# 240 rows to an expert, weight pieces set between the rows, block 1 gathered in the first MoE, single idle products

## The chip, the cores and the metric

The kernel runs on one core of a Trainium2 chip. The core has five engines that run side by side and wait for each other by semaphores: TensorE (PE; its weight loads are listed as PEld), VectorE (DVE), ScalarE (ACT), GpSimd (POOL) and SyncE (SP), from whose queue nearly all DMAs are issued; POOL issues the indexed ones. The metric is the device time of one launch in microseconds, as the median of a few runs.

## The reference

Three layers in a row over 3072 tokens (4 sequences of 768) of 384 numbers. Cut to what is computed:

```python
# gated linear attention, 8 heads of 48
state = f[:, :, t, :, None] * state + einsum('bhd,bhe->bhde', k[:, :, t], v[:, :, t])
y[:, :, t] = einsum('bhd,bhde->bhe', q[:, :, t], state)
# first MoE: 8 experts, 384 -> 1024 -> 384; a token goes to one expert or to none
do_compute = x @ w_skip > 0
e_idx = argmax(xc @ w_gate); gate_w = softmax(xc @ w_gate)[e_idx]
out[do_compute] = xc + gate_w * (maximum(xc @ w1[e], 0) @ w2[e])
# second MoE: dense, 384 -> 2048 -> 384
h = x @ w_in
g = where(h >= 1, h, where(h <= -1, 0, (h + 1) ** 2 / 4))
return g @ w_out
```

The weights of the second MoE arrive as 64-bit floats.

## The kernel before

Tokens stand in 24 tiles of 128 rows. Every float32 product that needs it is made of three fp32r products, high by high, high by low and low by high (`PASS`, `ORDER`), so that each operand is kept as an upper half (made by ACT) and a lower half (made by DVE or POOL as the difference).

Attention runs in an order written out by hand (`PLAN`). It ends with the routing of the last three tiles (21 to 23), one by one: logits on PE, choice of the expert on DVE, rank by PE, place on DVE. Meanwhile POOL has sent the rows of the earlier tiles by indexed DMA into `xs_d`, 256 rows (`CAP`) for each of 8 experts; a token whose rank in its expert is not under the limit is counted in `over`. Tokens of the first six tiles have a lower limit, 128 (`CAP0`), so that their rows stand in the first half of an expert's share. Ten calls of `warm` in the plan put products of the identity matrix on PE that nothing reads. At the end all engines read a flag (line 931): if a token is over the limit, a slow branch computes it; otherwise the branch is jumped over.

The first MoE (`moe1`) takes expert after expert: for 8 blocks of 128 hidden units nine products each (line 1132), streaming the expert's 256 rows; from PSUM ACT makes the upper half of h, DVE the lower (lines 1135, 1136); then for two tiles of 128 rows 24 products of 384 columns (line 1151), and ACT copies the result (`yo`), which goes to `yb_d`. The second MoE (`moe2`) takes blocks of three tiles, b = 0 to 7, twice: first the hidden blocks f = 0 to 7, then 8 to 15. A step (b, f) is nine products of layer 1 (line 1227), the bend by ACT and DVE into gh and gl, and, three steps later, nine products of layer 2 (line 1282).

All other work is strewn among these products by a clock of ticks: 16 in an expert, so 128 in the first MoE, and two in a step of the second. At a tick every job that runs does its next step, and its instructions go into the engines' queues, which keep their order. Three kinds of job matter here. `split_job` loads a piece of w1 or w2 (ACT line 251, DVE line 254). `widen_job` turns a piece of 384 columns of the 64-bit weights into float32: a load, `mag` on ACT (line 286), five DVE steps (lines 291 to 301), and then either a store, or the upper half by ACT (line 307) and the lower by POOL (line 311). Pieces of the second kind are the 20 of `DIRECT`; the list `direct` has the ticks at which they start, `direct_steps` at which tick after its start each of the six steps stands. `combine_job(b)` brings the expert's results back to the tokens of block b: an indexed gather by POOL (line 1181), gate and sum by DVE (line 1187), a store, a load in turned order, a 32x32 transpose by DVE (line 1202), upper half by ACT, lower half by POOL (lines 1208, 1212). `rows` has the steps of the second MoE at which it starts for b = 1 to 7. Block 0 is handled apart: its rows are gathered in the first MoE without the last expert (`base_job`), and the last expert's part is added through PE (`patch`), after the second layer's first tile of that expert.

Of the kernel before, what the change touches and what calls it, by code (L numbers as in the profile page):

```python
# [11 lines left out]
F32 = mybir.dt.float32  # L12
F32R = mybir.dt.float32r
# [17 lines left out]
CAP0 = 128  # L31
HOT = 21
# [25 lines left out]
    "rows": [0, 7, 15, 23, 31, 39, 47],  # L58
# [113 lines left out]
def gla_moe_kernel(ctx: ExitStack, tc: tile.TileContext, a: dict, out: bass.AP):  # L172
# [165 lines left out]
    def route_group(i0, n, ps_x, rt, tag, dense=False, cap=CAP, hot=None, ranks=None):  # L338
# [138 lines left out]
    def attention():  # L477
        with ExitStack() as es:
# [202 lines left out]
            def clear_rows(z):  # L681
                nc.sync.dma_start(z, zt[:z.shape[0]])
# [77 lines left out]
            for g, (i0, n) in enumerate(((0, 6), (6, 6), (12, 6), (18, 3), (21, 1), (22, 1), (23, 1))):  # L760
                job = route_group(i0, n, ps_x, rt, "x", cap=CAP if g else CAP0, hot=hot if i0 >= HOT else None,
# [251 lines left out]
    def moe1():  # L1013
        with ExitStack() as es:
# [5 lines left out]
            def load_x(e):  # L1020
                if e >= E:
                    return
                xg_t[e] = [mx.tile([128, DM], F32, tag="xg", name="xg", bufs=XG) for t in range(2)]
                for t in range(2):
                    nc.sync.dma_start(xg_t[e][t], xs_d[CAP * e + 128 * t:CAP * e + 128 * t + 128, :])

            def prep_x(e):
                xg = xg_t.pop(e)
                xh, xl = xhl[e] = x_pair(hp_, CAP)
                for t in range(2):  # L1030
                    tp = ps_t.tile([128, 3, 128], F32, tag="tp", name="tp")
                    for c in range(3):
                        T.transpose(tp[:, c], xg[t][:, 128 * c:128 * (c + 1)], ident)
                    sl = slice(128 * t, 128 * t + 128)
                    A.activation(xh[:, :, sl], tp, AF.Copy)
                    V.tensor_tensor(out=xl[:, :, sl], in0=tp, in1=xh[:, :, sl].bitcast(F32), op=ALU.subtract)
# [74 lines left out]
            agenda.setdefault(MTUNE["select"], []).append(select_job)  # L1111
            for i in range(TB):
# [9 lines left out]
            for e in range(E):  # L1122
# [4 lines left out]
                hs = [hp_.tile([128, 8, CAP], F32R, tag=f"h{z}", name=f"h{z}") for z in range(2)]  # L1127
# [18 lines left out]
                for t in range(2):  # L1146
# [12 lines left out]
                    A.activation(yo, op, AF.Copy)  # L1159
                    store = lambda e=e, t=t, yo=yo: nc.sync.dma_start(  # L1160
                        yb_d[CAP * e + 128 * t:CAP * e + 128 * t + 128, :], yo)
# [5 lines left out]

    def moe2():
        NF = F2 // 128
        with ExitStack() as es:  # L1170
            gp = es.enter_context(tc.tile_pool(name="gp", bufs=2))
            gs, ops, post = {}, {}, []

            def combine_job(b):
                tiles, t = range(TB * b, TB * (b + 1)), {}

                def gather(i):
                    t["g", i] = mx.tile([128, DM], F32, tag="xg", name="xg", bufs=XG)  # L1180
                    G.indirect_dma_start(
                        out=t["g", i], out_offset=None, in_=yb_d[:, :],
                        in_offset=IndirectOffsetOnAxis(slot[:, i:i + 1], 0),
                        bounds_check=ROWS, oob_is_err=False)

                def add(i):
                    V.scalar_tensor_tensor(out=rows(i), in0=t["g", i], scalar=gate[:, i:i + 1],
                                           in1=rows(i), op0=ALU.mult, op1=ALU.add)

                def store(i):  # L1190
                    nc.sync.dma_start(xt_d[i], rows(i))

                def load(i):
                    r = t["r", i] = stg.tile([128, PIECE], F32, tag="raw", name="raw")
                    src = xt_d[i].rearrange("(I t) (r k) -> r t I k", t=32, r=4)
                    for k in range(4):
                        nc.sync.dma_start(r[32 * k:32 * k + 32, :DM].rearrange("t (I k) -> t I k", I=4), src[k])

                def blocks(i):
                    r = t["r", i]  # L1200
                    t["x", i] = r[:, DM:].rearrange("p (c t) -> p c t", c=3)
                    V.transpose(out=t["x", i].rearrange("p c (I t) -> p I c t", t=32),
                                in_=r[:, :DM].rearrange("p (I j c) -> p I c j", I=4, c=3))

                def hi(i):
                    if i % TB == 0:
                        turned(b, gp if b % 4 else mx)
                    A.activation(xhl2[b][0][:, i % TB], t["x", i], AF.Copy)

# [178 lines left out]
```

## Time and profile before

| | us |
|---|---|
| median of 3 runs (lowest, highest) | 714.44 (713.12, 716.37) |
| profiled execution, its own time | 720.89 |
| span in the profile, first to last instruction | 719.1 |
| PE busy | 684.0 (95%) |
| DVE busy | 497.9 (69%) |
| ACT busy | 440.3 (61%) |
| POOL busy | 140.4 (20%) |
| attention and routing, to the first product of the first MoE | 0 to 161.1 |
| first MoE, to the first product of the second | 161.1 to 309.9 |
| second MoE, to the last product | 309.9 to 715.5 |

A share of busy time is an average over stages. Products on PE are pipelined: the recorded length of one (0.28 to 0.34 us) is longer than the distance to the next, so the pace is read from runs of products in the chain of waits, not from the mean of one. "[1.22 <-DVE h L1136]" behind a row is the engine's idle time ahead of it and what ended it. A wait for several things is put down to the one that came last by the profile, and a DMA can hide behind the engine that is named.

### The profile page before, as it was taken

Reading aid. Unit: us, or ns where it says so; the run is one execution under the profiler, and the core shown is the slowest. Engines: PE = TensorE matmul, PEld = TensorE weight load, DVE = VectorE, ACT = ScalarE, POOL = GpSimd, SP = SyncE. Lnnn points to the kernel's source line nnn. Section 1 sums busy time; section 2 is a strip of 40 time slices with the busy share of each in tenths; the row PEclk is TensorE's granted clock in tenths of the full one; section 3 lists DMA queues with packets and bytes.
Section 4 is the critical chain, followed back from the end, with each engine's and each line's share of the span. In section 5 each row is a group of like instructions: output and inputs, shape, how many; then the busy total and the mean of one; then the engine's idle time right before and its main releaser. Section 6 shows DMA issues by size and latency. Waiting matters only on the chain.

```text
span 719.1 us, 14223 instructions
## 1 busy us (share of the span) xinstructions
PE 684.0 (95%) x5281; PEld 650.7 (90%) x5281; DVE 497.9 (69%) x1001; ACT 440.3 (61%) x921; POOL 140.4 (20%) x154
## 2 busy tenths in 40 slices
PE   3999999879999999899999999999999999999997
PEld 2777777679999999899899999899999999999997
DVE  6999889765899878886677787676534444444443
ACT  5888776525666666556666667676555455454553
POOL 2251644421000000333324422431100000000000
PEclk9999999999999999999999999999999999999999
DMA  8998795026799878445644555553131212202210
GB/s 230 314 305 272 258 304 173 34 86 226 273 310 327 286 253 285 147 120 145 187 125 139 169 152 148 160 160 138 67 99 66 91 42 71 95 0 67 67 64 35
DMA packets 79867, 116.68 MB, mean 162 GB/s; under 512 B 18316, under 2 KB 60095, under 8 KB 79794
## 3 DMA queue, kind: packets, MB, share of 16 engines
q1 hardware_dynamic: 75570, 104.30, 44.2%
q0 software_dynamic: 4224, 11.45, 5.3%
q8 instruction: 42, 0.69, 0.4%
q14 instruction: 31, 0.25, 0.1%
HBM read 86.77 MB, written 31.66 MB: 165 GB/s over the span
## 4 chain that ended last, share of the span: by engine, by line
PE 62%; DVE 8%; ACT 3%; DMA 2%; issue 2%; SPq 0%; DVEq 0%; ACTq 0%
PE hp L1227 24%; PE op L1282 15%; PE tp L1282 10%; PE op L1151 6%; PE hp L1132 6%; DVE wlb L254 1%; DMA r<-in_w_in_dram 1%; DVE gl L1255 1%; DVE e L299 1%; DVE w L292 1%; DMA raw<-in_w_dram 1%; DVE wla L254 1%; DVE h L1136 1%; ACT q L1235 1%; ACT gh L1254 1%
## 5 line engine op out<-in xcount | busy, mean ns | idle before, releaser
L1255 DVE TENSOR_TENSOR gl<-q,gh 128x384 fp32r<-128x384 f32 x128 | 73.8, 576 | 137.4 <-ACT gh L1254 135.3
L1235 ACT ACTIVATE q<-hp 128x384 f32<-128x384 f32 x96 | 46.8, 488 | 79.5 <-PE hp L1227 75.0
L1254 ACT ACTIVATE gh<-q 128x384 fp32r<-128x384 f32 x128 | 67.0, 523 | 20.6 <-DVE q L1248 20.5
L1227 PE MATMUL hp<-xh,wha 128*128 128x384 f32 x192 | 64.2, 335 | 0.0
L1227 PE MATMUL hp<-xh,wla 128*128 128x384 f32 x192 | 64.1, 334 | 0.0
L1227 PE MATMUL hp<-xh,whb 128*128 128x384 f32 x192 | 64.1, 334 | 0.0
L1227 PE MATMUL hp<-xh,wlb 128*128 128x384 f32 x192 | 64.1, 334 | 0.0
L1248 DVE COPY_PREDICATED q<-mask,hp 128x384 f32<-128x384 int32 x96 | 56.8, 592 | 0.0
L1236 ACT ACTIVATE mask<-hp,minus 128x384 f32<-128x384 f32 x96 | 55.4, 577 | 0.0
L1242 ACT ACTIVATE q<-q 128x384 f32<-128x384 f32 x96 | 50.2, 523 | 0.0
L532 POOL TENSOR_TENSOR k<-k,ip 128x512 f32<-128x512 f32 (+1 forms) x26 | 30.9, 1204 | 66.7 <-DVE ip L523 40.0
L1227 PE MATMUL hp<-xl,wha 128*128 128x384 f32 x192 | 43.6, 334 | 0.0
L1227 PE MATMUL hp<-xl,whb 128*128 128x384 f32 x192 | 43.6, 334 | 0.0
L1282 PE MATMUL op<-wha,gh 128*128 128x384 f32 x120 | 40.5, 338 | 1.6 <-ACT gh L1254 0.9
L1282 PE MATMUL op<-wha,gl 128*128 128x384 f32 x120 | 40.7, 339 | 0.9 <-DVE gl L1255 0.9
L1282 PE MATMUL op<-wla,gh 128*128 128x384 f32 x120 | 40.1, 335 | 0.0
L1282 PE MATMUL op<-whb,gl 128*128 128x384 f32 x120 | 40.1, 334 | 0.0
L1282 PE MATMUL op<-whb,gh 128*128 128x384 f32 x120 | 40.1, 334 | 0.0
L1282 PE MATMUL op<-wlb,gh 128*128 128x384 f32 x120 | 40.1, 334 | 0.0
L1135 ACT ACTIVATE h<-hp 128x256 fp32r<-128x256 f32 x64 | 24.2, 383 | 24.1 <-PE hp L1132 23.9
L1132 PE MATMUL hp<-x,whb 128*128 128x256 f32 x192 | 34.8, 280 | 1.8 <-DVE h L1136 1.8
L1227 PEld LDWEIGHTS hp<-xh,wha 128*128 128x128 f32 x192 | 36.0, 188 | 0.3 <-issue 0.2
(237 smaller groups left out, 1960.0 us busy)
## 6 DMA issues: line engine op xcount, KB each, us to landing
raw<-in_w_dram SPq DMA_DIRECT2D x64, 384.0 KB, 5.7
r<-in_w_in_dram SPq DMA_DIRECT2D x16, 384.0 KB, 4.1
r<-in_w_out_dram SPq DMA_DIRECT2D x16, 384.0 KB, 6.5
f<-in_fT_dram SPq DMA_DIRECT2D x10, 512.0 KB, 5.8
k<-in_kT_dram SPq DMA_DIRECT2D x10, 512.0 KB, 7.7
q<-in_qT_dram SPq DMA_DIRECT2D x10, 512.0 KB, 6.2
v<-in_vN_dram SPq DMA_DIRECT2D x10, 512.0 KB
xl<-xl SPq DMA_DIRECT2D x8, 576.0 KB
```

The lines of the kernel that those rows point to most:

```text
L532: (G if u else V).tensor_tensor(out=d["k"][:, p], in0=d["k"][:, p], in1=d["ip"][:, p], op=ALU.mult)
L1132: T.matmul(hp, w1[wi][:, DM * f + 128 * c:DM * f + 128 * c + 128], x2[xi][:, c], start=(n == 0), stop=(n == 8))
L1135: A.activation(hs[0][:, f], hp, AF.Relu)
L1151: T.matmul(op, hs[hi][:, f, 128 * t:128 * t + 128], w2[wi][:, DM * f:DM * (f + 1)], start=(n == 0), stop=(n == 23))
L1227: T.matmul(hp.rearrange("p (t k) -> p t k", t=TB), w[wi][:, DM * (f % 8) + 128 * c:DM * (f % 8) + 128 * c + 128], xhl2[b][xi][:, :, c], st ...
L1235: A.activation(q, hp, AF.Relu, bias=1.0)
L1236: A.activation(mask, hp, AF.Relu, bias=minus)
L1242: A.activation(q, q, AF.Square, scale=0.5)
L1248: V.copy_predicated(q, mask.bitcast(I32), hp)
L1254: post.append((lambda: A.activation(gh, q, AF.Copy), lambda: V.tensor_tensor(out=gl, in0=q, in1=gh.bitcast(F32), op=ALU.subtract)))
L1255: lambda: V.tensor_tensor(out=gl, in0=q, in1=gh.bitcast(F32), op=ALU.subtract)))
L1282: T.matmul(ops[b][t], g2[gi][:, 128 * t:128 * t + 128], w[wi][:, DM * (f % 8):DM * (f % 8 + 1)], start=(f == f0 and n == 0), stop=(f == f1 ...
```

## The change

- `USED = 240` is the new limit of rows in an expert. Layer 1 of the first MoE streams 240 columns, the second tile of an expert has 112 rows in its load, transposes, products, copy and store. The spacing of the experts' rows in memory stays 256. Eight small DMAs on SP's queue clear the rows of `yb_d` that are no longer written.
- `direct`, `direct_steps`: other ticks for the 64-bit pieces. Of the first four one moves from tick 107 to 114 and one from 120 to 119; the later sixteen stand three to a block's 16 ticks, not one every 7 ticks; the upper and lower half come one tick later after the DVE steps.
- `combine_job(1)` starts at tick 125 of the first MoE and not at the first step of the second. Its gather leaves out the rows from 1920 on (the second tile of the last expert), and a memset clears its target first. Its transposes stand 11 ticks after the gather, not 9.
- `warm` issues one product, not two.

```diff
-    "direct_steps": [0, 5, 6, 7, 8, 9],
+    "direct_steps": [0, 5, 6, 7, 9, 10],
-    "direct": [104, 107, 120, 126] + [140 + 7 * k for k in range(16)],
+    "direct": [104, 114, 119, 126] + [143 + 16 * (k // 3) + (0, 5, 9)[k % 3] for k in range(16)],
-    "rows": [0, 7, 15, 23, 31, 39, 47],
+    "rows": [7, 15, 23, 31, 39, 47],
+    "rows1": 125,
+    "rows1_steps": [0, 4, 4, 5, 11, 12, 13],
...
             def clear_rows(z):
+                if z.shape[0] == 1:
+                    for e in range(E):
+                        clear_rows(yb_d[CAP * e + USED:CAP * (e + 1), :])
                 nc.sync.dma_start(z, zt[:z.shape[0]])
...
-                for n in range(2):
-                    T.matmul(idle[0][:, 128 * n:128 * n + 128], ident, ident, start=True, stop=True)
+                T.matmul(idle[0][:, :128], ident, ident, start=True, stop=True)
...
+            agenda.setdefault(MTUNE["rows1"], []).append(lambda: combine_job(1))
...
-                    hp = ps_1.tile([128, CAP], F32, tag="hp", name="hp")
+                    hp = ps_1.tile([128, USED], F32, tag="hp", name="hp")
...
-                        T.matmul(hp, w1[wi][:, DM * f + 128 * c:DM * f + 128 * c + 128], x2[xi][:, c],
+                        T.matmul(hp, w1[wi][:, DM * f + 128 * c:DM * f + 128 * c + 128], x2[xi][:, c, :USED],
...
-                            T.matmul(op, hs[hi][:, f, 128 * t:128 * t + 128], w2[wi][:, DM * f:DM * (f + 1)],
+                            T.matmul(op[:nr], hs[hi][:, f, 128 * t:128 * t + nr], w2[wi][:, DM * f:DM * (f + 1)],
...
+            n = ROWS + 1
+            if b == 1:
+                n = ROWS - CAP + CAP0
+                G.memset(t["g", i], 0.0)
             G.indirect_dma_start(
-                        out=t["g", i], out_offset=None, in_=yb_d[:, :],
+                out=t["g", i], out_offset=None, in_=yb_d[:n, :],
                 in_offset=IndirectOffsetOnAxis(slot[:, i:i + 1], 0),
-                        bounds_check=ROWS, oob_is_err=False)
+                bounds_check=n - 1, oob_is_err=False)
...
-            starts = {s: b for b, s in enumerate(MTUNE["rows"], 1)}
+            starts = {s: b for b, s in enumerate(MTUNE["rows"], 2)}
```

On DVE, in the first layer of the last expert (h is its lower half, the rows with w_ and e_ are a 64-bit piece's steps, wla_<-raw and wlb_<-raw other lower halves of weights), before:

```order
L1136 SCALAR_TENSOR_TENSOR h_6219<-hp,h_6218 128x256
L291 TENSOR_SCALAR w_6235<-w_6235 128x384
L292 SCALAR_TENSOR_TENSOR w_6235<-r_6160,w_6235 128x384
L294 TENSOR_SCALAR e_6258<-w_6235 128x384
L984 TENSOR_TENSOR wla_6110<-raw,wha_6109 128x384
L1136 SCALAR_TENSOR_TENSOR h_6219<-hp,h_6218 128x256
L299 SCALAR_TENSOR_TENSOR e_6258<-r_6160,e_6258 128x384
L301 TENSOR_TENSOR w_6235<-w_6235,e_6258 128x384
L254 TENSOR_TENSOR wlb_5980<-raw,whb_5979 128x768
L1136 SCALAR_TENSOR_TENSOR h_6219<-hp,h_6218 128x256
```

And in the changed kernel, from the last h on (x_134<-xg,gate,x_134 is block 0's sum, xg<-pp the patch):

```order
L1144 SCALAR_TENSOR_TENSOR h_6215<-hp,h_6214 128x240 x2
L1092 SCALAR_TENSOR_TENSOR x_134<-xg,gate,x_134 128x384
L991 TENSOR_TENSOR wla_6213<-raw,wha_6212 128x384
L1092 SCALAR_TENSOR_TENSOR x_134<-xg,gate,x_134 128x384
L296 TENSOR_SCALAR w_6342<-w_6342 128x384
L297 SCALAR_TENSOR_TENSOR w_6342<-r_6272,w_6342 128x384
L299 TENSOR_SCALAR e_6366<-w_6342 128x384
L304 SCALAR_TENSOR_TENSOR e_6366<-r_6272,e_6366 128x384
L306 TENSOR_TENSOR w_6342<-w_6342,e_6366 128x384
L991 TENSOR_TENSOR wla_6213<-raw,wha_6212 128x384 x3
L1112 TENSOR_TENSOR xg<-pp,xg 128x384 x3
```

The five steps of one piece have moved from among the h to behind the last of them.

On POOL, from the gathers for block 0 (xg<-yb_d in line 1079, 1086 after) to those of block 1 (line 1181, 1190 after); wla_6110<-w_ and wla_6108<-w_ are 64-bit pieces' lower halves. Before:

```order
L1079 DMA xg<-yb_d,slot 128x384 x2
L311 TENSOR_TENSOR wla_6110<-w_6235,wha_6109 128x384
L1181 DMA xg<-yb_d,slot 128x384
L311 TENSOR_TENSOR wla_6110<-w_6461,wha_6109 128x384
L1181 DMA xg<-yb_d,slot 128x384 x2
L311 TENSOR_TENSOR wla_6110<-w_6549,wha_6109 128x384
```

Now:

```order
L1086 DMA xg<-yb_d,slot 128x384
L316 TENSOR_TENSOR wla_6108<-w_6342,wha_6107 128x384
L1189 MEMSET xg 128x384
L1190 DMA xg<-yb_d,slot 128x384
L1189 MEMSET xg 128x384
L1190 DMA xg<-yb_d,slot 128x384
L1189 MEMSET xg 128x384
L1190 DMA xg<-yb_d,slot 128x384
L316 TENSOR_TENSOR wla_6108<-w_6428,wha_6107 128x384
L316 TENSOR_TENSOR wla_6108<-w_6566,wha_6107 128x384
```

Block 1's three gathers have moved ahead of two of the pieces' lower halves, each behind a memset.

On ACT, in block 1's steps of the second MoE (whb_<-w_ is a 64-bit piece's upper half, w_<-r_ its `mag`, the q and gh rows the bend of one step). Before:

```order
L286 ACTIVATE w_6792<-r_6698 128x384
L1235 ACTIVATE q<-hp 128x384
L1236 ACTIVATE mask<-hp,minus 128x384
L1254 ACTIVATE gh<-q 128x384
L1242 ACTIVATE q<-q 128x384
L307 ACTIVATE whb_6355<-w_6792 128x384
L1235 ACTIVATE q<-hp 128x384
```

Now:

```order
L291 ACTIVATE w_6847<-r_6758 128x384
L1252 ACTIVATE q<-hp 128x384
L1253 ACTIVATE mask<-hp,minus 128x384
L1271 ACTIVATE gh<-q 128x384
L1259 ACTIVATE q<-q 128x384
L1309 ACTIVATE o<-op 128x384 x2
L1271 ACTIVATE gh<-q 128x384
L1261 ACTIVATE q<-q,half 128x384
L1217 ACTIVATE xh_6932<-raw 128x384
L312 ACTIVATE whb_6347<-w_6847 128x384
L1252 ACTIVATE q<-hp 128x384
```

Between a piece's `mag` and its upper half there was one step's bend; now the next step's copies and its bend stand there too.

## Rows read from the trace of the kernel before

**Rows 1.** The page, busy times, and the group of gl: busy, mean ns, idle.

```profile
PE 684.0 (95%) x5281; PEld 650.7 (90%) x5281; DVE 497.9 (69%) x1001; ACT 440.3 (61%) x921; POOL 140.4 (20%) x154
...
L1255 DVE TENSOR_TENSOR gl<-q,gh 128x384 fp32r<-128x384 f32 x128 | 73.8, 576 | 137.4 <-ACT gh L1254 135.3
```

**Rows 2.** Chain of waits in order of time: start, us, what ran.

```profile
215.90 8.41 PE hp L1132 x72
224.30 0.66 PE tp L1033 x6
...
319.03 1.56 PE hp L1227 x9
...
709.27 6.26 PE op L1282 x36
```

**Rows 3.** PEld in order of time, and line 656: ns shortest, median, longest.

```profile
81.94 0.30 PEld L656 LDWEIGHTS lp<-fold,lt 128*128 128x128 f32 x2
...
L656 PEld LDWEIGHTS lp<-fold,lt x48: 186/189/337, 30.4 to 153.3; 128*128 128x128 f32 x48
```

**Rows 4.** PE at the end of attention: start, us, instruction, [idle before].

```profile
149.53 2.05 PE L795 MATMUL idle<-ident 128*128 128x128 f32 x16
151.51 0.42 PE L627 MATMUL lp<-xt,wp 128*32 128x128 f32 x8
...
152.36 1.06 PE L795 MATMUL idle<-ident 128*128 128x128 f32 x8
153.25 0.29 PE L656 MATMUL lp<-fold,lt 128*128 128x9 f32 x2
...
161.09 0.36 PE L1132 MATMUL hp<-raw,wha 128*128 128x256 f32 x1 [2.11 <-DVEq L931]
```

**Rows 5.** ACT in the same stretch.

```profile
149.66 0.60 ACT L609 ACTIVATE xt<-yy 128x512 f32<-128x512 f32 x1 [1.66 <-PE yy L604]
152.00 0.28 ACT L638 ACTIVATE lt<-lp 128x128 f32<-128x128 f32 x1 [1.74 <-PE lp L627]
```

**Rows 6.** DVE in the same stretch.

```profile
153.57 0.17 DVE L380 TENSOR_REDUCE m<-lp 128x1 f32<-128x8 f32 x1 [0.63 <-PE lp L656]
```

**Rows 7.** PE in the first MoE, products after a wait.

```profile
168.96 0.39 PE L1132 MATMUL hp<-raw,wha 128*128 128x256 f32 x1 [1.22 <-DVE h L1136]
...
295.44 0.38 PE L1132 MATMUL hp<-x,whb 128*128 128x256 f32 x1 [1.75 <-DVE h L1136]
```

**Rows 8.** Two stretches: length, busy us by engine, granted clock, DMA share, GB/s.

```profile
135.00:142.00 7.00, 6.61 (x87) 5.38 (x88) 4.95 (x19) 3.27 (x10) 0.00 (x0) 0.76 0.05 16
...
215.00:233.00 18.00, 18.00 (x132) 18.00 (x131) 16.67 (x32) 11.47 (x22) 0.00 (x0) 1.00 0.90 325
```

**Rows 9.** PE in the second MoE: its first product, and three after a wait.

```profile
309.89 0.35 PE L1227 MATMUL hp<-xh,wha 128*128 128x384 f32 x1
...
317.55 0.44 PE L1282 MATMUL op<-wha,gl 128*128 128x384 f32 x1 [0.70 <-DVE gl L1255]
...
344.69 0.44 PE L1282 MATMUL op<-wha,gh 128*128 128x384 f32 x1 [0.72 <-ACT o L1292]
...
459.13 0.45 PE L1282 MATMUL op<-wha,gh 128*128 128x384 f32 x1 [0.89 <-ACT gh L1254]
```

**Rows 10.** DVE, two slow steps.

```profile
291.90 1.69 DVE L299 SCALAR_TENSOR_TENSOR e<-r,e 128x384 f32<-128x384 uint32 x1
...
315.66 1.83 DVE L1255 TENSOR_TENSOR gl<-q,gh 128x384 fp32r<-128x384 f32 x1 [0.65 <-ACT gh L1254]
```

**Rows 11.** ACT, upper halves of 64-bit pieces after a wait.

```profile
294.21 0.52 ACT L307 ACTIVATE wha<-w 128x384 fp32r<-128x384 f32 x1 [3.17 <-DVE w L301]
...
342.06 0.53 ACT L307 ACTIVATE whb<-w 128x384 fp32r<-128x384 f32 x1 [2.34 <-DVE w L301]
```

**Rows 12.** POOL, the first gather for block 1.

```profile
315.00 1.02 POOL L1181 DMA_INDIRECT xg<-yb_d,slot  x1 [18.02 <-DVE q L1250]
```

**Rows 13.** SP's queue: a clear; and its waits in total, times, longest.

```profile
68.72 0.34 SPq L682 DMA_DIRECT2D yb_d<-zt  x1
...
SPq L511 <- DVE q L551: 18.4, 5, 7.9
```

More of the change, by code (lines that the diff above doesn't have):

```diff
@@ L31 @@
 CAP0 = 128
+USED = 240
 HOT = 21
@@ L1126, in moe1 @@
                 x2 = xhl.pop(e)
-                hs = [hp_.tile([128, 8, CAP], F32R, tag=f"h{z}", name=f"h{z}") for z in range(2)]
+                hs = [hp_.tile([128, 8, USED], F32R, tag=f"h{z}", name=f"h{z}") for z in range(2)]
                 for f in range(8):
-                    hp = ps_1.tile([128, CAP], F32, tag="hp", name="hp")
+                    hp = ps_1.tile([128, USED], F32, tag="hp", name="hp")
                     n = 0
                     for c, wi, xi in ORDER:
-                        T.matmul(hp, w1[wi][:, DM * f + 128 * c:DM * f + 128 * c + 128], x2[xi][:, c],
+                        T.matmul(hp, w1[wi][:, DM * f + 128 * c:DM * f + 128 * c + 128], x2[xi][:, c, :USED],
                                  start=(n == 0), stop=(n == 8))
@@ L1145, in moe1 @@
                     ps_h.append(ctx.enter_context(tc.tile_pool(name="ps_o1", bufs=1, space=PSUM)))
-                for t in range(2):
+                for t, nr in enumerate((128, USED - 128)):
                     op = ps_o.tile([128, DM], F32, tag="op", name="op")
@@ L1166, in moe1, with combine_job, gather, add @@
                 issue_weights(e + 2, 1)
+    pools = {}
+    def combine_job(b):
+        tiles, t = range(TB * b, TB * (b + 1)), {}
+        def gather(i):
+            t["g", i] = mx.tile([128, DM], F32, tag="xg", name="xg", bufs=XG)
+            n = ROWS + 1
+            if b == 1:
+                n = ROWS - CAP + CAP0
+                G.memset(t["g", i], 0.0)
+            G.indirect_dma_start(
+                out=t["g", i], out_offset=None, in_=yb_d[:n, :],
+                in_offset=IndirectOffsetOnAxis(slot[:, i:i + 1], 0),
+                bounds_check=n - 1, oob_is_err=False)
+        def add(i):
+            V.scalar_tensor_tensor(out=rows(i), in0=t["g", i], scalar=gate[:, i:i + 1],
+                                   in1=rows(i), op0=ALU.mult, op1=ALU.add)
+        def store(i):
+            nc.sync.dma_start(xt_d[i], rows(i))
+        def load(i):
+            r = t["r", i] = stg.tile([128, PIECE], F32, tag="raw", name="raw")
+            src = xt_d[i].rearrange("(I t) (r k) -> r t I k", t=32, r=4)
+            for k in range(4):
+                nc.sync.dma_start(r[32 * k:32 * k + 32, :DM].rearrange("t (I k) -> t I k", I=4), src[k])
+        def blocks(i):
+            r = t["r", i]
+            t["x", i] = r[:, DM:].rearrange("p (c t) -> p c t", c=3)
+            V.transpose(out=t["x", i].rearrange("p c (I t) -> p I c t", t=32),
+                        in_=r[:, :DM].rearrange("p (I j c) -> p I c j", I=4, c=3))
+        def hi(i):
+            if i % TB == 0:
+                turned(b, pools["gp"] if b % 4 else mx)
+            A.activation(xhl2[b][0][:, i % TB], t["x", i], AF.Copy)
+        def lo(i):
+            xh, xl = (z[:, i % TB] for z in xhl2[b])
+            G.tensor_tensor(out=xl, in0=t["x", i], in1=xh.bitcast(F32), op=ALU.subtract)
+            if i % TB == TB - 1:
+                keep_low(b)
+        ticks = MTUNE["rows1_steps" if b == 1 else "rows_steps"]
+        steps = [[] for _ in range(ticks[-1] + TB)]
+        for fn, t0 in zip((gather, add, store, load, blocks, hi, lo), ticks, strict=True):
+            for k, i in enumerate(tiles):
+                steps[t0 + k].append(lambda fn=fn, i=i: fn(i))
+        return [lambda fns=fns: [fn() for fn in fns] for fns in steps]
     def moe2():
@@ L1171, in moe2 @@
             gp = es.enter_context(tc.tile_pool(name="gp", bufs=2))
+            pools["gp"] = gp
             gs, ops, post = {}, {}, []
[L1176 to L1181, printed above, removed]
-                        out=t["g", i], out_offset=None, in_=yb_d[:, :],
-                        in_offset=IndirectOffsetOnAxis(slot[:, i:i + 1], 0),
-                        bounds_check=ROWS, oob_is_err=False)
[L1186 to L1208, printed above, removed]
-                def lo(i):
-                    xh, xl = (z[:, i % TB] for z in xhl2[b])
-                    G.tensor_tensor(out=xl, in0=t["x", i], in1=xh.bitcast(F32), op=ALU.subtract)
-                    if i % TB == TB - 1:
-                        keep_low(b)
-                steps = [[] for _ in range(MTUNE["rows_steps"][-1] + TB)]
-                for fn, t0 in zip((gather, add, store, load, blocks, hi, lo), MTUNE["rows_steps"], strict=True):
-                    for k, i in enumerate(tiles):
-                        steps[t0 + k].append(lambda fn=fn, i=i: fn(i))
-                return [lambda fns=fns: [fn() for fn in fns] for fns in steps]
```

26 lines of the change are left out of this document (13 added, 13 removed).

## The prediction

> **What bounds the kernel now.** I read the page first: TensorE is busy 684.0 of 719.1 us [rows 1], so the question is where it is not, and what those holes hang on. The chain of waits gives the pace when nothing is in the way. In the first MoE the nine products that make one tile of h (line 1132) come 72 to an expert in 8.41 us, 116.8 ns each at 256 columns; six transposes of 128 columns take 0.66 us, 110 ns each; in the second MoE nine products of 384 columns take 1.56 us, 173.3 ns each [rows 2]. From its first product at 309.89 to the end of the chain's last run of products (709.27 + 6.26 = 715.53) the second MoE lasts 405.6 us; 256 groups of 1.56 us make 399.4. So its products lose 6.3 us to waits, which no single row shows as a whole; three of the places are at 317.55, 344.69 and 459.13, with 0.70, 0.72 and 0.89 us of idle engine [rows 9]. In the first MoE there are two large holes: 1.22 us before 168.96 and 1.75 us before 295.44, both waiting for VectorE's lower half of h [rows 7]. Ahead of that, the start of the first MoE at 161.09 waits 2.11 us for the flag that all engines read at line 931; that flag ends a serial chain through PE, ACT and DVE that routes the last three tiles [rows 4 to 6].
>
> **The change part by part.** The sum is made in the profiled execution: span 719.1 us, its own time 720.89 us. That is 6.45 us above the 714.44 us median of the three timed runs; I subtract the same microseconds from the median.
>
> A, idle products single. A call of warm issued two f32 products, four instructions; now two. Four calls stand between sq23 and logit23: 16 instructions, first at 149.53, and logit23 starts at 151.51 [rows 4]. What logit23 needs, the copy xt, was done at 149.66 + 0.60 = 150.26 [rows 5]. With 8 instructions gone, half of 1.98 us, logit23 starts near 150.5: 1.0 us sooner. Two more calls stand before route_fold23: 8 instructions from 152.36 to 153.25, 0.89 us, while its operand lt was ready at 152.28 [rows 4, 5]; half of that is 0.45 us. DVE waits for just this product, 0.63 us at 153.57, and starts the last tile's choice of expert from it [rows 6]. So A = -1.5 us. Bounds: -1.9 if the two calls at 145.5 are worth the same 0.45 us, and +1.7 (second rival).
>
> B, 240 columns. 576 products of line 1132 (72 x 8) stream 240 columns, not 256. By the straight line through 116.8 ns at 256 and 173.3 at 384 [rows 2], a column is 0.441 ns, 16 are 7.1 ns, and 576 x 7.1 = 4.1 us. Against that stands the stationary operand, still 128 columns, whose load precedes each product: two loads with a product of 9 columns take 0.30 us, the second alone 0.189, so they start 0.11 us apart [rows 3]; and the transposes, 128 columns both ways, do not go under 110 ns [rows 2]. So the pace at 240 lies between 110 and 116.8 ns; the 110 row is the nearer one, as only the load remains to set it, and I put 2 ns on it: 112. 576 x 4.8 = 2.8 us. About 0.4 us of that is swallowed: in the first two experts PE waits anyhow for h, on a DVE that is behind with weight pieces (1.22 us at 168.96 [rows 7]), and gets no earlier release from faster products. From 215 to 233 us DVE is busy 16.67 of 18.00 us and DMA 0.90 [rows 8], enough air for an expert that is 0.35 us in 17.4 shorter. B = -2.4, bounds -4.1 and 0. The second layer streams 384 columns as before, with 112 stationary columns for the second tile: no change.
>
> [...]
>
> C, one piece moved off the last expert's first layer (direct tick 107 to 114). Before 295.44 PE waits 1.75 us for h. DVE had spent its time on this piece's five steps, among them one of 1.69 us at 291.90, and ACT stood 3.17 us before its upper half at 294.21 [rows 7, 10, 11], with three h behind it. Now the five steps come after the last h. What hides them there is the second layer, which needs no further h; late next is the yo copy before the patch, since ACT's upper half of the piece stands ahead of it. C = -1.5, bounds -1.8 and 0.
>
> D, the second MoE. Three edits with one answer. A piece's upper half is issued two ticks after DVE's last step, not one: at 342.06 ACT stood 2.34 us on that step [rows 11] and the products 0.72 us after it [rows 9]. Block 1's rows are gathered from tick 125 on, without the last tile of expert 7; now POOL waits 18.02 us to 315.00 [rows 12], which I read as the landing of expert 7's last store although the row names DVE, and the gathers fall upon the first gl of the stage, which takes 1.83 us where its group's mean is 0.58 [rows 1, 10]; PE pays 0.70 at 317.55. The 20 pieces stand between the rows' transposes. Against it: three pieces in 16 ticks, not 2.3, so each 25 us hold 0.7 pieces more of five DVE steps. The three waits named, with the slowed products behind each, are about half of the 6.3 us; I take that 4 of it go and 1.4 come back elsewhere: D = -2.6. Bounds: -5.5, and +3.0, three new waits of the size at 344.69 with the slowed products behind each.
>
> E, eight more clears on SP's queue, 0.34 us each [rows 13], 2.7 us ahead of the loads of q, v, f and k. SP waits there on DVE, 18.4 us in five waits, one of 7.9 [rows 13]; that takes it up. 0, with +0.5 if one load is late.
>
> Sum: -1.5 - 2.4 - 1.5 - 2.6 = -8.0 us, so 706.4 (712.9 in a profiled run). Own range of this case, most bounds not met together: 701 to 711.
>
> **The rivals.** First, the waits of the second MoE come back: D is +3.0. For it: DVE's denser diet, and that a queue in program order passes each late transfer on to gl. Against it: the worst waits are of just the kind that is loosened. -1.5 - 2.4 - 1.5 + 3.0 = -2.4: 712.0 us.
>
> [...]
>
> Third, slower: products under 256 columns lose their pace. Every fp32r product in this trace has 256 columns or 384; the narrower ones are plain f32, two instructions each, 16 instructions in 2.05 us [rows 4]: 0.256 us for 128 columns, 2.0 ns a column against 0.46 at 256. If 240 columns fell to that pace, a product would take 480 ns, 576 x 363 = 209 us, 918 with the other terms. It decides from the first expert on: the other terms are worth 5.6 us, 9.7 ns a product, so any pace above 127 ns makes the change slower. Against it: the pace goes smoothly from 384 to 256, and the 110 ns of narrow transposes show that load and stream keep up.
>
> Fourth, it doesn't do what it says: an expert with over 240 rows sends all engines into the branch that is jumped over now. By the same rows, 24 f32 products of 128 columns (6.1 us) and 8 of 384 at twice 173 ns (2.8 us), for 24 tiles and 8 experts, are 1.7 ms. The reference's inputs put at most 219 rows on one expert, so it gets little.
>
> **How the numbers follow.** Forecast 0.68, first rival 0.18, second 0.07, third 0.05, fourth 0.02. Half a percent, about what a measurement of this kernel can tell from no change, is 3.6 us: under 710.9 faster, over 718.0 slower. Faster: nearly all of the forecast, some of rivals one and two: 0.75. Same: most of rival one: 0.15. Slower: rivals three and four and a bad tail of one: 0.10. The range 700 to 714 takes in the forecast, rival two and most of rival one.
>
> **What would show it.** A: logit23 within 1 us of sq23's end, and no second dip of the clock before the first MoE. B: 72 products in 8.0 to 8.1 us; 8.4 would make it 0, over 9.1 the third rival. C: no hole over 0.5 us in the last expert's first layer. D: from the first product of the second MoE to the last, 402 to 404 us; 408 is the first rival. Wrong altogether: the flag's branch taken, or new holes before the patch.

## The result and the profile after

| | before | after |
|---|---|---|
| median of 4 runs, us (lowest, highest) | 714.83 (713.12, 716.37) | 705.15 (704.1, 706.21) |
| ratio, 95% interval | | 0.9865 (0.984 to 0.9891) |
| profiled execution, its own time | 720.89 | 704.16 |
| span | 719.1 | 702.4 |

The change took 9.7 us; 8.0 were forecast (706.4 us). The profiled execution of before lies 6 us over its median, so the two profiles are compared by stages, not by spans; the differences below rest on this one profile of before. A stage runs from the first product of one to the first product of the next; "xt to m" runs from the start of ACT's last copy xt to DVE's first step of the last tile's choice, the link that the idle products sit on. "Experts 4 to 6" is the time of each of them.

| us | before | after | difference |
|---|---|---|---|
| xt to m (149.66 to 153.57; 141.31 to 143.89) | 3.91 | 2.58 | -1.33 |
| first expert | 19.08 | 19.93 | +0.85 |
| experts 2 and 3 together | 35.57 | 34.34 | -1.23 |
| experts 4 to 6, each | 17.41 | 17.11 | -0.30 |
| last expert | 23.73 | 23.69 | -0.04 |
| second MoE, to its last product | 405.6 | 400.15 | -5.5 |

The page, against [rows 1]: PE is busy 10.1 us less, the others are as busy as before within 2.5 us, and the idle time ahead of gl is smaller.

```profile
PE 673.9 (96%) x5261; PEld 645.3 (92%) x5261; DVE 499.0 (71%) x1001; ACT 437.8 (62%) x921; POOL 141.1 (20%) x157
...
L1272 DVE TENSOR_TENSOR gl<-q,gh 128x384 fp32r<-128x384 f32 x128 | 72.4, 566 | 133.3 <-ACT gh L1271 133.0
```

The chain of waits of after, start, us, what ran, against [rows 2]: 72 products of an expert take 8.06 us in place of 8.41, and the run that ends the second MoE is as long as before, 6.26.

```profile
197.40 8.43 PE op L1159 x48
205.83 8.06 PE hp L1140 x72
213.89 0.62 PE tp L1040 x6
...
692.55 6.26 PE op L1299 x36
```

In before the 48 products of the second layer had taken 8.34 us, which no row has shown so far; the same view of before:

```profile
224.96 8.34 PE op L1151 x48
```

The end of attention in after, on PE, ACT and DVE, against [rows 4 to 6]: start, us, engine, instruction, idle time before it.

```profile
141.18 1.16 PE L802 MATMUL idle<-ident 128*128 128x128 f32 x8
142.27 0.42 PE L632 MATMUL lp<-xt,wp 128*32 128x128 f32 x8
...
151.40 0.54 PE L1140 MATMUL hp<-raw,wha 128*128 128x240 f32 x1 [2.11 <-DVEq L938]
```

```profile
141.31 0.60 ACT L614 ACTIVATE xt<-yy 128x512 f32<-128x512 f32 x1 [1.87 <-PE yy L609]
```

```profile
143.89 0.17 DVE L385 TENSOR_REDUCE m<-lp 128x1 f32<-128x8 f32 x1 [0.19 <-PE lp L661]
```

logit23 now starts 0.36 us after the copy xt has ended at 141.91, where it was 1.25; DVE waits 0.19 us for the folded logits, not 0.63.

PE around the patch in after. The hole of 1.75 us in the last expert's first layer [rows 7] is gone, but ahead of the transposes of block 0's sums (line 1098) and of the patch (line 1111) stand 0.62 and 1.66 us; before, the patch waited 0.32. Then comes the second MoE's first product.

```profile
285.91 0.58 PE L1098 MATMUL tp<-ident,x 128*128 128x128 f32 x3 [0.62 <-DVE x L1092]
292.24 3.41 PE L1111 MATMUL pp<-sel,yo 128*128 128x128 f32 x18 [1.66 <-ACT yo L1167]
...
298.65 0.34 PE L1244 MATMUL hp<-xh,wha 128*128 128x384 f32 x1
```

The chain of waits says what the patch waited for: the last expert but one is stored, a gather is issued and lands after 6.10 us, DVE adds, takes the moved piece's five steps, ACT its upper half (line 312) and that of another weight piece (line 987), and only then comes the copy yo, which the patch reads.

```profile
275.74 2.09 DMA yb_d<-yo
...
280.66 6.10 DMA xg<-yb_d,slot
...
287.87 0.53 DVE x L1092
288.39 0.28 DVE w L296
...
290.28 0.57 DVE w L306
...
290.88 0.03 ACT wha L312
...
291.31 0.51 ACT wha L987
291.81 0.39 ACT yo L1167
...
292.24 3.42 PE pp L1111 x18
```

In the second MoE the waits of ACT by line tell the difference. The columns: line waited for, us in total, times, longest. Of before, then of after:

```profile
ACT q L1244 <- DVE q L1238: 18.5, 25, 1.3
ACT whb L307 <- DVE w L301: 17.8, 15, 2.3
ACT wha L307 <- DVE w L301: 3.6, 2, 2.3
```

```profile
ACT q L1261 <- DVE q L1255: 31.0, 31, 2.7
...
ACT wha L312 <- DVE w L306: 1.7, 1, 1.7
```

ACT stood 21.4 us, in 17 waits, ahead of the upper halves of 64-bit pieces; now 1.7 in one. Part of this standing has only moved: ahead of the bend's q, a step that waits for DVE's step of the same bend, it is 31.0 us for 18.5. But PE doesn't pay for that: after 303.83, where PE waits 0.34 us, no product of the second MoE starts over 0.45 us after the one before it.

### The profile page after: what moved, and what is told of

The parts are those of the page before. It is cut to its first block, busy times and chain, and to the rows that moved or that the text cites. A ratio compares the mean times of both kernels' runs of the same rounds, so it can differ in the third digit from the quotient of the medians.

```text
span 702.4 us, 14199 instructions
## 1 busy us (share of the span) xinstructions
PE 673.9 (96%) x5261; PEld 645.3 (92%) x5261; DVE 499.0 (71%) x1001; ACT 437.8 (62%) x921; POOL 141.1 (20%) x157
## 4 chain that ended last, share of the span: by engine, by line
PE 73%; DVE 2%; DMA 1%; ACT 1%; issue 1%; POOL 0%; ACTq 0%; POOLq 0%; DVEq 0%
PE hp L1244 28%; PE op L1299 18%; PE tp L1299 11%; PE op L1159 8%; PE hp L1140 8%; DMA xg<-yb_d,slot 1%; PE tp L1040 1%; PE pp L1111 0%; DVE wlb L259 0%; ACT whb L256 0%; DMA yb_d<-yo 0%; DVE wla L991 0%; DVE w L297 0%; DVE xl L1115 0%; DVE e L304 0%
## 5 line engine op out<-in xcount | busy, mean ns | idle before, releaser
L1143 ACT ACTIVATE h<-hp 128x240 fp32r<-128x240 f32 x64 | 23.6, 370 | 25.1 <-PE hp L1140 25.1
L1261 ACT ACTIVATE q<-q,half 128x384 f32<-128x384 f32 x32 | 19.8, 618 | 31.0 <-DVE q L1255 31.0
L1144 DVE SCALAR_TENSOR_TENSOR h<-hp,h 128x240 fp32r<-128x240 f32 x64 | 24.6, 402 | 17.9 <-ACT h L1143 17.9
```

What stands on the lines that cost most here:

```text
L1144: V.scalar_tensor_tensor(out=hs[1][:, f], in0=hp, scalar=0.0, in1=hs[0][:, f].bitcast(F32), op0=ALU.max, op1=ALU.subtract)
```

## The experiments

The single edits and some of the undone edits (u_256, u_lag, u_107, i_224) ran where the kernel before takes 729 us and not 715. Most of the difference lies ahead of the first rank of the last tiles (rank of tile 21): with two idle products it starts at 149.6 to 151.7 us there and at 138.6 in f_two. Why is not known. So ratios are compared, and the stages of the table above. No kernel leaves out part of the computation.

**One idle product alone** (a_single).

```diff
-                for n in range(2):
-                    T.matmul(idle[0][:, 128 * n:128 * n + 128], ident, ident, start=True, stop=True)
+                T.matmul(idle[0][:, :128], ident, ident, start=True, stop=True)
```

> The kernel before with one idle product instead of two, nothing else changed. Theory one (the serial chain of the last tiles' routing got shorter, and of the 9.7 us by which the first MoE starts earlier in the profile after, the rest is what the profiled execution of before, 6.45 us over its median, lost by chance in attention): the median falls by 1.5 to 2.3 us, logit23 starts within 1 us of sq23's end, the first MoE starts near 153 us. Theory two (the whole 9.7 us belong to the change): the first MoE starts near 151.4 and the time falls by 5 us or more. Theory three (the clock drops on the first products of the first MoE, since PE ran thin ahead of them, and this takes the gain back): the nine first products take 2.2 us, and the median moves by less than 0.5 us.

Measured: 725.72 us against 729.25, ratio 0.9949 (0.9931 to 0.9967), 3.5 us. The link:

```profile
155.60 0.60 ACT L609 ACTIVATE xt<-yy 128x512 f32<-128x512 f32 x1 [1.66 <-PE yy L604]
```

```profile
158.17 0.17 DVE L380 TENSOR_REDUCE m<-lp 128x1 f32<-128x8 f32 x1 [0.19 <-PE lp L656]
```

158.17 - 155.60 = 2.57 us, as in after. The first nine products ran at the low clock here too (granted 0.66 from 165 to 170 us, first expert 20.03 us), so theory three's premise holds and its conclusion doesn't: the median fell. It fell more than the link's 1.3 us and more than theory one said; from the rank of tile 21 to the first MoE it takes 15.5 us, the three other single edits 16.9. The first MoE starts at 165.7 here and at 166.5 to 168.6 in those, so none of the starts that theories one and two gave came.

**240 rows alone** (b_240): the diff's lines with `USED`, and nothing else.

> The kernel before with 240 rows of an expert used, clears included; two idle products, the old ticks, block 1 gathered in the second MoE. Theory one (a product's pace follows the columns down to the load of 128): 72 products in 8.06 us, 576 products 2.8 us quicker, of which the second layer with its 112 stationary columns and DVE's weight pieces take back 0.4 to 1.2: the median falls by 1.6 to 2.4 us. Theory two (the wider gain at the start of the first MoE comes from the eight clears, which hold SP's loads back): the first MoE also starts 3 us or more earlier than in the kernel before. Theory three (DVE is the bound in the first MoE): no gain, within 0.5 us.

Measured: 727.17 against 729.25, ratio 0.9966 (0.9951 to 0.9982), 2.1 us. Experts 4 to 6 take 17.11 us, the second MoE 405.4. The first MoE starts at 168.6, no earlier than in its neighbours: theory two falls, and the median is in theory one's range. But the first MoE as a whole takes 147.91 us, only 0.9 less than in before.

**The two lists of ticks alone** (c_ticks).

```diff
-    "direct_steps": [0, 5, 6, 7, 8, 9],
+    "direct_steps": [0, 5, 6, 7, 9, 10],
-    "direct": [104, 107, 120, 126] + [140 + 7 * k for k in range(16)],
+    "direct": [104, 114, 119, 126] + [143 + 16 * (k // 3) + (0, 5, 9)[k % 3] for k in range(16)],
```

> The kernel before with only the two lists of ticks of the 64-bit pieces changed. Theory one: the waits in the second MoE hang on the upper halves that are issued one tick after DVE's last step, so these lists alone take it from 405.6 to about 401.5 us, and the 1.75 us hole in the last expert's first layer is traded for one before the patch: the median falls by 4 us. Theory two: the waits hang on block 1's late rows, which pass their lateness on from queue to queue: the second MoE stays above 404 us and the median falls by 1 us or less.

Measured: 723.46 against 729.25, ratio 0.9915 (0.9888 to 0.9941), 5.8 us. The second MoE takes 400.16 us: these two lists together are worth the whole 5.5. The hole in the last expert's first layer is gone, and ahead of the transposes and of the patch PE idles 1.14 and 1.42 us: theory one.

**Block 1's rows in the first MoE alone** (d_rows1): the diff's `rows`, `rows1` and `combine_job`, with 256 rows.

> The kernel before with only block 1's rows gathered in the first MoE (256 rows to an expert, two idle products, the old ticks of the pieces). Theory one (ticks carry the gain of the second MoE): only the waits near its start go, 0.7 + 0.3 us and the slowed products behind them, the second MoE takes 404 us and the median falls by 1 to 1.5 us. Theory two (block 1's late rows carry it): the second MoE takes 401 us or less and the median falls by 4 us or more.

Measured: 726.15 against 729.25, ratio 0.9958 (0.9941 to 0.9976), 3.1 us. The second MoE takes 403.65, 2.0 less than before. The 2.0 and the 5.5 of c_ticks are largely the same waits, since together they give 5.5.

**The changed kernel again** (after_again).

> The changed kernel as it stands, a second time, beside the single edits, to see whether they add up. In these runs the kernel before takes 729 us, about 14 us more than in the first comparison, nearly all of it ahead of the first rank of the last tiles. Theory one (the stages from there on carry the change: tail of the routing -2.3, first MoE -1.6, second MoE -5.5): it is 9.4 us under the kernel before, and these three stages last within 0.5 us of what they last in the first profile of after. Theory two (the four edits add up as single medians, -3.5, -2.1, -5.8 and -3.1): it is 14.5 us under it.

Measured: 704.89 against 714.65, ratio 0.9867 (0.9852 to 0.9882), 9.8 us. The kernel before took 715 us this time, so the comparison with the single edits goes by ratios: theirs sum to 2.1%, this one is 1.3%. They don't add up; the waits of the second MoE that two edits share account for 2.0 of the 5.7 us between, and the rest stays open. Theory one's 9.4 us is near: from the rank of tile 21 to the first MoE it is 14.5 us, as in the first profile of after, and the second MoE takes 400.15 to the hundredth; the first MoE is 0.9 us shorter (146.37 for 147.25). For here the granted clock stays at 1.00 at the start of the first MoE, where in after it is 0.50 from 152 to 154 us, though the same instructions and the same wait of 2.11 us for the flag lead up to it; the first expert takes 18.93 us, not 19.93. The first MoE starts at 151.40 in after and at 153.31 here, where the granted clock is 1.00 from 155 to 158 us too. Length, busy us by engine, granted clock, DMA share, GB/s; in after, then here:

```profile
150.00:155.00 5.00, 3.60 (x18) 3.64 (x19) 1.14 (x3) 1.19 (x3) 2.38 (x3) 0.66 0.07 25
```

```profile
150.00:155.00 5.00, 2.89 (x26) 2.71 (x25) 1.39 (x5) 1.15 (x3) 1.29 (x2) 1.00 0.03 10
```

**Two idle products in the changed kernel** (f_two): the edit of a_single turned round.

> The changed kernel with two idle products again. Theory one (the products stand in the serial chain; the clock's drop on the first products of the first MoE costs 1.0 us in the first expert, which the next two give back because VectorE has caught up with its pieces): the stretch from the first rank to the first MoE takes 16.8 us and not 14.5, the first expert 18.9 and not 19.9, the two after it 0.4 to 1.6 us more together; the median rises by 2 us. Theory two (the drop costs what the shorter chain gains): no difference, within 0.7 us.

Measured: 707.68 us, ratio to before 0.9908 (0.9894 to 0.9921): 2.8 us over after_again. The link:

```profile
143.28 0.60 ACT L614 ACTIVATE xt<-yy 128x512 f32<-128x512 f32 x1 [1.66 <-PE yy L609]
```

```profile
147.19 0.17 DVE L385 TENSOR_REDUCE m<-lp 128x1 f32<-128x8 f32 x1 [0.63 <-PE lp L661]
```

3.91 us, to the hundredth the link of before. The stretch from the first rank to the first MoE is 16.1 us, not the 16.8 expected; after_again has 14.5. The rest of the 2.8 stands in this profile in the second expert (18.26 for 17.23) and in the last (24.57 for 23.81). Neither can be laid to the idle products: g_late, with single ones, takes 18.95 in its second expert, and in the last expert of f_two the granted clock fell behind the hole (0.66 from 297 to 302 us).

**Block 1's rows in the second MoE again** (h_rows0): d_rows1 turned round in the changed kernel.

> The changed kernel with block 1's rows gathered in the second MoE again. Theory one (with the new ticks the second MoE has no wait left that block 1's rows could take away, and the first MoE doesn't depend on them): the second MoE takes 400.2 us, the last expert 23.7, the median stays within 0.7 us. Theory two (the three gathers have to be out of the way): the waits near the start of the second MoE come back, it takes 401.5 us, and the median rises by 1.3 us or more.

Measured: 706.31, ratio 0.9891 (0.9876 to 0.9906): 1.4 us over after_again. The second MoE takes 401.15, with one wait back at the place of [rows 9], where it was 0.70. By the median it is theory two. But c_ticks, which gathers block 1's rows in the second MoE too, takes 400.16 with the new ticks: there the late gathers cost nothing, and why they do here stays open.

```profile
306.49 0.44 PE L1298 MATMUL op<-wha,gl 128*128 128x384 f32 x1 [0.63 <-DVE gl L1271]
```

**The holes before the patch** (g_late): the piece and block 0's sums later by a tick.

```diff
-    "direct": [104, 114, 119, 126] + [143 + 16 * (k // 3) + (0, 5, 9)[k % 3] for k in range(16)],
+    "direct": [104, 115, 119, 126] + [143 + 16 * (k // 3) + (0, 5, 9)[k % 3] for k in range(16)],
-    "base0": [110, 112, 117, 121],
-    "base1": [111, 113, 119, 122],
-    "base2": [112, 114, 120, 123],
+    "base0": [110, 112, 118, 122],
+    "base1": [111, 113, 120, 123],
+    "base2": [112, 114, 121, 124],
```

> The changed kernel with the moved piece one tick later still (115, so that its upper half stands behind the copy yo that the patch waits for) and the sums and transposes of block 0's rows one tick later. Theory one (the holes of 0.96, 0.33 and 1.99 us before the patch come from the order of ACT's and PE's queues behind a late gather): two thirds of them go, the last expert takes 21.7 us and not 23.7, the median falls by 1.5 to 2 us. Theory two (whatever the order, the patch can't start before the gather that lands 6.1 us after its issue and DVE's steps behind it): the hole only moves, and the median stays within 0.7 us.

Measured: 702.39, ratio to before 0.9838 (0.9818 to 0.9859): 2.5 us under after_again, the fastest of the kernels where before takes 715: theory one, by more than it said. The last expert takes 20.93 us. Which of the two moves does it was not run apart. The chain runs through PE without a hole, first layer, second layer with the transposes strewn in, patch; yo stands ahead of the piece's upper half on ACT:

```profile
275.49 8.07 PE hp L1140 x72
283.56 3.16 PE op L1159 x18
286.72 0.34 PE tp L1098 x3
287.06 1.07 PE op L1159 x6
...
289.88 3.40 PE pp L1111 x18
```

```profile
289.32 0.48 ACT L1167 ACTIVATE yo<-op 128x384 f32<-128x384 f32 x1
...
291.13 0.52 ACT L312 ACTIVATE wha<-w 128x384 fp32r<-128x384 f32 x1 [0.72 <-DVE w L306]
```

**256 rows in the changed kernel** (u_256): `USED = 256`, no clears.

> The changed kernel with 256 rows of an expert used again (no clears). Theory one (the pace): 72 products go from 8.06 back to 8.41 us, experts 3 to 5 from 17.11 to 17.41, the last expert stays at 23.7 to 24.1 since its holes hang on a late gather and not on PE, and the median rises by 2 to 2.4 us. Theory two (clears and shorter rows matter beside the pace, ahead of the first MoE): the first MoE starts 1 us later besides, and the median rises by 3 us or more. Theory three (DVE is the bound): within 0.7 us.

Measured: 720.73 against 729.41, ratio 0.9895 (0.9872 to 0.9918). Beside the 0.9867 of after that is 0.0028, 2.0 us; the intervals overlap. Experts 4 to 6 are back at 17.41. That is theory one's size. The last expert takes 25.01 us, not the 23.7 to 24.1 expected; a stretch of low clock (0.66 from 308 to 313 us) follows the hole before the patch.

**Only the steps of a piece as before** (u_lag).

```diff
-    "direct_steps": [0, 5, 6, 7, 9, 10],
+    "direct_steps": [0, 5, 6, 7, 8, 9],
```

> The changed kernel with only the steps of a 64-bit piece as before: the upper half one tick after the last of DVE's steps, the lower half two. Theory one (the waits of the second MoE came from ACT standing on this step): they come back, the second MoE takes 403 us or more in place of 400.2, the median rises by 3 us. Theory two (they came from the pieces' ticks, which stood 7 apart and so ran into the rows' transposes, and are now 16 to a group of three): the second MoE stays under 401 us and the median within 0.7 us.

Measured: 727.72 against 729.41, ratio 0.9977 (0.9957 to 0.9997): of the gain hardly 2 us are left. The second MoE takes 408.5 us, 8.3 more than after and 2.9 more than before: theory one, at more than twice its size. The nearest kernel with the old ticks is d_rows1, which gathers block 1's rows early as this one does and has the old steps: 403.65 us, so with the old steps the new ticks cost 4.8. ACT's waits in it, and PE behind one of them:

```profile
ACT whb L312 <- DVE w L306: 21.9, 14, 1.9
...
ACT wha L312 <- DVE w L306: 6.1, 2, 3.8
```

```profile
379.18 0.44 PE L1299 MATMUL tp<-wha,gh 128*128 128x384 f32 x1 [1.11 <-ACT o L1309]
```

**The moved piece put back** (u_107): `direct` with 107 in place of 114.

> The changed kernel with the piece that moved from tick 107 to 114 put back to 107, nothing else. Theory one (the move only traded the hole in the last expert's first layer for one of the same size before the patch): a hole of 1.3 to 1.9 us among the first layer's products, the hole before the patch's products under 0.7 us and not 1.99, the last expert within 0.4 us of 23.8, the median within 0.7 us. Theory two (the move was worth the 1.5 us of the forecast and the holes before the patch come from the gather alone): both kinds of hole, the last expert 25 us or more, the median 1.3 us higher.

Measured: 719.63 against 729.41, ratio 0.9875 (0.9847 to 0.9903), no different from after. The hole is back in the first layer, and the one before the patch is gone:

```profile
297.86 0.38 PE L1140 MATMUL hp<-x,whb 128*128 128x240 f32 x1 [2.13 <-DVE h L1144]
307.33 3.40 PE L1111 MATMUL pp<-sel,yo 128*128 128x128 f32 x18 [0.33 <-ACT yo L1167]
```

The last expert takes 25.21 us, as theory two had it; but up to 1.7 of that is the clock, by an estimate that takes it as 0.50 while it was down, as after has it from 152 to 154 us, where products start 0.21 us apart and not 0.11. It was down for (5 x 0.24 + 5 x 0.10) / 0.5 = 3.4 us behind the hole, and half of that is 1.7:

```profile
296.00:301.00 5.00, 3.14 (x15) 3.14 (x16) 5.00 (x7) 1.56 (x5) 3.24 (x3) 0.76 0.47 150
301.00:306.00 5.00, 5.00 (x31) 5.00 (x30) 3.20 (x8) 1.41 (x4) 0.42 (x1) 0.90 0.01 3
```

Without it 23.5 or a little more are left; before and after take 23.7. The median speaks for theory one, the profile's last expert by itself for two; by the pair of holes I take theory one.

**224 rows in g_late** (i_224).

```diff
-USED = 240
+USED = 224
```

> The kernel with the later piece and the later sums and transposes (702.4 us), now with 224 rows of an expert used. Theory one (the straight line goes on): from 116.8 ns at 256 columns and 112.0 at 240 a product takes 107 ns, 72 products 7.7 us, and the time falls by 576 x 4.8 = 2.8 us less some tenths. Theory two (a load of 128 stationary columns sets the pace from here, 110 ns by the starts of two loads in a row and the transposes): 72 products take 7.9 us or more, and the time falls by 1.2 us or less. Theory three (weight pieces on DVE set the first MoE's pace by then): the first two experts wait 1 us more, and nothing is left of the gain.

Measured: 714.04 against 729.41, ratio 0.981 (0.9783 to 0.9838), beside g_late's 0.9838: nothing that the intervals tell apart. The products:

```profile
217.07 8.03 PE hp L1140 x72
225.10 0.58 PE tp L1040 x6
225.68 8.43 PE op L1159 x48
```

8.03 / 72 = 111.5 ns. From 256 to 240 columns the pace fell by 4.8 ns, from 240 to 224 by 0.4: theory two by the pace. Its reason, the load, is not shown. Three of the six transposes in a group have the narrower second tile: the six take 0.66 us with 128 columns there, 0.62 with 112, 0.58 with 96, so one of the narrow ones takes about 97 and 83 ns, though its load still has 128 stationary columns, of 112 and 96 rows. So 128 stationary columns by themselves don't hold a product at 110 ns. This kernel has the lowest ratio of all, and fits these inputs by 5 rows (at most 219 in an expert).

## Why the prediction was right

The time, 705.15 for 706.4, came from three of the forecast's four mechanisms, but not with its sizes. That it came so near is luck in part: C's 1.5 us did not come, and D brought 2.9 us more than forecast. By stages against the one profile of before, from the rank of tile 21 to the first MoE it is -2.3 us (16.8 to 14.5), the first MoE -1.55, the second -5.5, together -9.3; 9.7 and 9.8 were measured.

**A, forecast -1.5, measured -1.3 in its link.** Twelve f32 instructions less in the serial chain, eight ahead of logit23 and four ahead of route_fold23, are worth nearly what the rows said: the link takes 3.91 us in all five profiles with two idle products and 2.57 in all nine with one. From the rank of tile 21 to the first MoE, like against like, it is 1.4 (a_single) and 1.6 us (f_two). The medians give it more, 3.5 and 2.8 us; where the surplus comes from stays open.

**B, forecast -2.4, measured -0.30 in each of experts 4 to 6, and -2.0 to -2.1 by the medians.** Eight times -0.30 would be the forecast's -2.4. The pace of 112 ns came out to the tenth, and i_224 shows hardly less at 224 columns, 111.5 ns. That the load sets this pace, as the forecast took it, is not shown, and the narrower transposes put its second witness in doubt. The second layer, costed at no change, takes 8.43 and not 8.34 us an expert, +0.7 for eight, and not in its narrower tile alone: the median distance of its products went from 173 to 175 ns in both tiles. Whether the first experts swallow 0.4 us can't be read: the first three together take 54.6 us in before, 54.8 in b_240, and 53.3 to 55.0 in the eight profiles with 240 rows.

**C, forecast -1.5, measured about nothing: the step that failed.** The last expert takes 23.69 us in after and 23.81 in after_again, against 23.73 in before and 23.85 in b_240, which has the old ticks with 240 rows; and u_107, with the piece put back, has after's ratio within its interval. The sign that the prediction named came, no hole over 0.5 us in the first layer, and the gain did not. I said that the second layer hides the moved steps, that the copy yo before the patch is late next, and gave that copy 0.3 us of the 1.8. It took all: ahead of the transposes and the patch PE idles 0.62 + 1.66 us, where it had idled 1.75 + 0.32 in the first layer and at the patch. What the step left out is what stood ahead of the moved piece on DVE: a sum that waits for a gather issued only after the last store of the expert before. g_late, which lets yo and the transposes pass, is worth 2.5 us and has no hole there. So my "new holes before the patch" came, as a mark of an altogether wrong prediction, and only cost one term.

**D, forecast -2.6, measured -5.5, at the end of its bounds.** The mechanism was right: an upper half issued one tick after DVE's last step makes ACT stand in front of the bend [rows 11]. The second MoE took 400.15 us, under the 402 to 404 that the prediction named as its sign. The size was off twice. I counted the three waits that single rows showed, about half of 6.3 us, though 17 waits of this kind made 21.4 us on ACT; a view of waits by line would have said so. And I let 1.4 us come back for the denser pieces, which did not come back where the upper half is issued a tick later. With the old steps they would: u_lag's second MoE takes 4.8 us more than d_rows1's. The later steps with the old ticks were not run, so the 5.5 belong to both lists together. Block 1's gathers, which I had as a cause of equal rank, are worth 2.0 us by themselves (d_rows1) and 0 to 1.0 beside the new ticks: without them 400.16 (c_ticks) and 401.15 (h_rows0), with them 400.15.

**E, forecast 0.** b_240 starts the first MoE at 168.6 us, the two other single edits with two idle products at 166.5 and 167.2; with one profile of each, neither a gain nor a loss by the clears is shown.

**The rivals.** The first, waits that come back, is what u_lag is, with 408.5 us for its 408: it depended on one tick, which the change had set. The second, another stretch of low clock like the one in before (granted 0.50 from 137 to 140 us, 0.76 from 135 to 142 [rows 8]), did take place, and more than once: such a stretch stands in the first expert in six of the nine profiles with single idle products (after, 0.66 from 150 to 155 us; a_single, 0.66 from 165 to 170; h_rows0, u_256, u_lag, u_107) and in none of the five with two. The +1.7 us that stands for it in the bounds of A is an estimate, half of a stretch of 3.4 us at 0.50, and no run shows it. What the runs showed is less: in after 1.0 us in the first expert (19.93 for after_again's 18.93), where PE's wait for h late in the first layer is 0.98 us and not 1.50; that VectorE, busy with weight pieces there, catches up while PE is slow is my reading of it. The medians fell all the same. No run here shows why the same instructions met the low clock in after and not in after_again. The third fell: 112 ns in experts 4 to 6, not over 127. Of the fourth there is no trace: the jump over the branch ends a wait of 2.11 us as before.

## What to carry to other kernels

When a queue keeps its order, don't ask only how long a step takes but who stands behind it when it waits: with the pieces in their new places, one tick between a producer's last step and its consumer was worth 8.3 us of the second MoE (u_lag against after), while moving a whole piece out of a hole was worth nothing that the runs can tell. Count such waits by a view that sums them by line, not by the worst rows. And before work is moved to a place "with nothing after it", follow what that place itself waits for, here a gather's landing.

## What the runs showed of the hardware

- fp32r products with 128 stationary columns came 116.8, 112.0 and 111.5 ns apart at 256, 240 and 224 streamed columns (72 in 8.41, 8.06 and 8.03 us, in before, after and i_224), and 173.3 at 384: 4.8 ns less from 256 to 240, 0.4 less from 240 to 224. Plain f32 transposes did not stop there: about 110, 97 and 83 ns at 128, 112 and 96 columns, an estimate from groups of six (0.66, 0.62 and 0.58 us in the same three), each with a load of 128 stationary columns (of 128, 112 and 96 rows). What holds the products at 111.5 ns is not shown.
- Some holes were followed by low clock, others not. Twelve profiles have holes in the last expert, of 2.1 to 2.9 us together. In seven of them (c_ticks, d_rows1, f_two, h_rows0, u_256, u_lag, u_107) the granted clock was down for 3.4 us at 0.50 behind a hole (read as 0.66 over five us in f_two and u_256, as 0.76 and 0.90 over two times five in u_107), and the last expert takes 24.6 to 25.5 us; in five (before, after, after_again, a_single, b_240) it stayed at 1.00, and the last expert takes 23.7 to 24.2. The holes of u_256 (25.0) are those of after (23.7) to 0.02 us. g_late and i_224, without a hole, have no low clock there. So by an estimate from these times a hole with low clock behind it cost some 1 us above its length, and part of g_late's gain may be that.
- In after, an indexed gather of 128 rows landed 6.10 us after its issue (280.66 to 286.76), with the DMA engines busy 0.77 of that time; the median of the 24 gathers of that execution is 3.7.
